# A new order of all steps for the attention and feed-forward kernel, with new places, new engines and 46 instead of 44 warm-up products

## The chip, the core and the metric

The kernel runs on one core of a Trainium2 chip. The metric is the device time of one execution in microseconds (us). Inputs and outputs are float32 and lie in HBM. The engines are TensorE (PE in the profile; its weight loads are PEld), VectorE (DVE), ScalarE (ACT), GpSimd (POOL) and SyncE (SP), whose queue issues all transfers here.

## The reference

Eight batches of eight heads have 512 tokens and 32 states each, of 64 numbers. Tokens read from states and states from tokens, each by a softmax. The 544 rows per batch (512 token reads, 32 state reads), with the heads side by side, go through a feed-forward layer of 512 to 1024 to 512 with a softmax gate and a normalisation.

```python
def _attn_ref(x, state):                     # x (8,8,512,64), state (8,8,32,64)
    scores = scale * np.matmul(x, state.transpose(0, 1, 3, 2))
    ...                                      # softmax over the states
    xread = np.matmul(a, state)
    scores2 = scale * np.matmul(state, x.transpose(0, 1, 3, 2))
    ...                                      # softmax over the tokens
    sread = np.matmul(a2, x)
    return np.concatenate([xread, sread], axis=2)

def _moe_ref(x, w_in, w_out, g_ln):          # x (4352 rows, 512)
    h = x @ w_in
    sm = softmax(h)
    solu = h * sm
    ln = (solu - mu) / np.sqrt(var + 1e-06) * g_ln
    return (ln @ w_out).astype(np.float32)
```

The rows are 8 x 544 = 4352. The weights arrive as 64-bit floats.

## The kernel before

**Tiles.** The rows are cut into 34 tiles of 128: tile t below 32 is a quarter of the tokens of batch b = t // 4, and tiles 32 and 33 are the state reads of all batches. The matrix product of the token read with the states and that with `w_in` are joined: the states are first multiplied with `w_in`, and the token tiles then need one product with the result.

**Steps.** The work is written as named steps, each a generator that issues one instruction, or a few, at each turn:

- `l` loads a piece of a weight matrix, 512 KB; pieces 0 to 7 are `w_in` (piece 2c + n is quarter c, half n), 8 to 15 are `w_out`. `cl` (ACT) and `c` (three turns: DVE, DVE, then DVE or POOL) turn a piece into 32-bit floats. `wi` and `wo` split the weights into a high and a low part.
- `Ls` loads the states of four batches, `LT` and `Ln` load the tokens of a batch in two layouts.
- `V` b n multiplies the states of batch b with half n of `w_in` (`all_heads`, L191). It has two product turns, j = 0 and j = 1 (four heads and two quarters of `w_in` each), and two evictions. One product takes 64 rows and 32 columns of TensorE's array; the four of a turn use opposite corners, and those of j = 1 use the places that j = 0 leaves (`at = (q ^ j) * NS`).
- `S` b makes the scores of batch b by the same helper, j = 0 and j = 1 in one turn. `E` and `A` (`Ah` for batch 0, in two parts) are the two softmaxes; `R` is the read of the tokens, with two product turns, a scaling on DVE (`sr`, L423) that also frees the bank of the products, and a transposing product (L430).
- `Y`, `Z` and `P` keep a state product in DRAM, load it again and split it.
- `H` t makes the hidden row (L471): for tiles 0 to 3 in plain fp32 products, for the others in three products of split parts. `C` t is the softmax gate and the statistics; `D` t transposes it through DRAM (`ut`, `back`); `T` t splits it in four copies, `uh` and `ul` for each half; `O` t is the product with `w_out` (L539), the eviction with the scale (L546 on ACT, L548 on DVE) and the store. Tile 33 goes in two halves of 256 columns.
- `K` multiplies an identity with itself (L563). It computes nothing that is used and keeps TensorE at work while it would wait.

**What sets the order.** The string `ORDER` lists the steps turn by turn (`K*2` is two turns), and `issue` takes them one after the other. Each engine, and SP's queue of transfers, executes its own instructions in that order, so that an instruction that waits holds back all that is behind it on its engine. `OPT` says with one letter per step which engine does it (a ACT, d DVE, p POOL). `PLACES` gives each tile its buffer: `k4` are 45 buffers of 4 KB per partition that everything of that size shares, `t` four and `h` twice two banks of PSUM. A tile that takes a used buffer waits until the last reader of the one before is done.

In the old order TensorE's list begins with 15 warm-up products, then the first turn of `V30`, and ends the part with batch 0 (tiles 0 to 3) with the last step of `R0`; after that come the `H` of batch 1.

Of the kernel before, what the change touches and what calls it, by code (L numbers as in the profile page):

```python
# [28 lines left out]
OPT = dict(ph=2, k4=45, direct=[0, 1], hn=[0], vh=[0, 1], ah=[0], add='dddddpppppppdpdp', whi='aaaa', wlo='pdpp',
           ev='aaaaaaaaaaaaadaaaaaaaaaaaaaaaaaa', swh='aaaaaaaadaaaaaaa', swl='ppppdppdppdppdpd', sub='dppdddpd',  # L30
           subh='ppdddpdddpdddpdd', mulh='dpdddpdddpdddpdd', mul='ppddddpp', ath='aaaaadad', alo='dpdpdppp',
           up='aaaaaaaaadadadaaadadaaddadddaddada',
           uh='aaaadadaaaaaaaaaaaaaddaadaadaaaadaaaaadadaadaaaadadadddaaaddddaadaaa',
           ul='ddddppppdpppppdppppppdppdppdppppppdppdddpppppdppdpppddppdpdppddpdddd',
           oe='aaadaaaadaaaadaaaaaaaddddaaaaaaaaa', hs='aaaaaaaa', jit=[])
# [7 lines left out]
Ah01*2 V11 Ln00 E1*2 A1*3 P10 c9 H1*2 Ah01*2 E1 P11 Lg A1 Lg*2 V41*4 H0*2 C1*2 E1 Ah01 V51 Y71 Ah01 cl11 A1 K c11 E1
E0 C1*2 Lg Ah01 K C0 P11 E1 A1 K E1 C0 A1*2 Y41 Ln11 V51*2 H3 V51 H3 C0 D1 wo6 K Y31 cl15 LT20 C0*2 C3*2 P10 V61*2 A1
V61 A1 c11 A1 R0 c8 R0 D1 R0 l13 C0 H2 K H2 E1 K*2 V61 c15 E1 C3*3 D1 D0*2 C2 D3 K C2 S2 Ln10 wo0 wo1 R0*2 H4 C2 T1 E2
A2 E2 wo2 wo1 H4*4 E1 H4 wo3 wo0 E2 H5*2 wo3 D0 H5*2 wo2 H5*2 O1*3 R1*2 O1 T1 O1 D3 O1 T1 wo4 c13*2 C2 R0 cl13 D2 T0
Y40 O0 T0*2 wo4 O0*4 c13 wo5*2 O0 wo6 Y20 wo7*2 O0 T0 T1 E2 R1 D3 T3 A2*2 C2 C1 E2 D2 LT30 LT31 O1*3 O0*6 T3*2 O1*3 C1
O1 C4 T3 C4 O3*2 D2 O3 C3 A2 O1 O3 Y60 O3*2 C5 O3*2 C4 E2 C5*2 C4*2 C5 O3*2 D4 T2*3 O3*3 S3 Y21 T2 O0 D4 LT41 A2 E3
D5*2 E3 C4 E3*2 R1 H7*3 A2*2 H6*2 C2 D4 H6*4 C6*2 O2*2 Z21 O2*2 A2 H7 D5 A3 O2*8 H7 T4 O4*2 Y70 O4 Z20 T4*2 H7 T4 R1
O4 O3 O4 A3 Ln21 C6 O4*2 P21*2 O4*4 Ln20 O4 T5*3 A2 O2 A2 O5*3 E2*3 A2 O5*3 P20 LT40 C5 P20 C6 D6*2 C7 O4 A3 C7*2 H9*2  # L50
C5 H9*4 O5*2 C9 E3*2 O4 R1 E2 C7 D7 D6 Z30 Z31 D7 LT51 T5 O5*2 C9 O5*2 C9*2 D9*2 H8*2 O5 H8*4 S4 C8 C6*2 D7 O2 R2 Y51
R2 H10*3 R2 T6*4 Y50 O5 O6 P30*2 O6 E4 C8 H10 C8 E4 C8 A4 D9 E4*2 E3 Ln40 E4 O6*4 A3 D8*2 H10 Ln30 Z40 T7*2 H11*3 T7
O6*3 C7*2 H11*2 O6*2 P31 A3 E3*2 O6 T7 O6 H10 A3*2 O6 P31 O7*5 D8 E4 O7*3 C10 T9*3 C9*2 C10 T9 R2 C8 O7*2 A4 A3*2 H11
A3*2 A4 E4 R2 C8 O7*3 O9 LT50 R2 C10*2 T8 O9*2 C11*2 A4*2 O9*2 E3 D10 Z41 O9*7 Ln31 H13*3 O9 D10 C11*2 D11*2 T8*2 O7
T8 O9 H13*3 C13 C11*2 A4*2 D10 C13 Y61 C13 O8*8 C13 D13 C13 T10*2 H12*2 D11 Z51 T11 S5 T11 P51 T11 R3*2 A5*2 O8*4 R3
H15 H12*2 T10*2 Ln41 H15*3 O8*2 H12 E5*2 D13 H12 H15 C12*2 E5 O10*2 H15 P40 O10*2 E4 C10 O10*2 C12 C10 O10 P40 O10
O11*3 O10 A4 O10 O11 C12 E5*2 O10*3 D12 C12 H14*3 LT60 R3 A4 H14*3 T11 LT61 A4 D13 T13 E4 Ln61 C15 T13*3 A4 C12 O11*2
O10 D12 O11*4 C15 O11 Z50 O13*2 C15 P41 C15 Z61 C15 O11 A5 O13 D15 R3*2 O13*6 E5 P41 O11 C14 D12 E4 C14 E5*2 C14*2
Ln51 C13 T12 O13*4 H16 T12 P50 D14 T12 H16*5 S6 C16 R4 C16 P50 R4*2 O12*3 O11 D15 D14 D15 T15 D14 O12*5 C16 LT70 A5
T12 C16 O12*2 D16*2 H17 E5 A5*2 H17 O12 H17 O12 H18 H17*2 T15 E6 T15*2 C15 T14 E6 H17 O12 H18 A5 T14 E6*3 H18*2 O14*2  # L60
Z71 O14 T14 C17 D16 O14 O13 O15*2 O12 A6 O15*2 A6*2 H18 O14 P51 Ln50 H18 wi2 E5 C14 C17 O15 C17*2 D17 C17 O14*2 Z60
O15*2 O14*3 T14 O14*2 C16 C14 O14 H19*5 O15*3 A5 O15 A5 C16 T16*4 LT71 A5 C18 E6*2 C18*3 O15 H19 A5 C18 O15 E6 D18 R4
R5*2 R4 R5 O16*3 D17*2 O16*3 C19 O16*6 A6 H21*2 wi1 wi2 R4 H21 D18 C19*2 C17 H21 C19 H21 D19 O14 T17 P61 T17*2 S7 P61
E7 R5*3 D18 H21 O16 T18 H20 P60 H20 T18 O17*2 A6 O17*3 A7 C21*2 C19 D19 O17 Ln70 O17*3 P71 A6*2 E6 C21 A7 C21 D21 D19
T19 O15 E7*3 H20*2 O18 D21 O18*2 O17 T17 O17*2 T18 T19 T18 T19 O18*2 C18 P60 C21 O17*2 C21 H20*2 T19 O18 C20 H22 A7
C20 E7*2 C20*2 A6*2 E6 D21 H22*5 O19*2 T21*2 O18*5 C20 C19 O19*3 Z70 H23 O18 H23 O19 D20 O19 O18 D20 T21 O19*2 O18
A7*2 C22 T21 C22*3 A6 D20 T20 O21 O19*3 O21 D22 H23 D22*2 T20*3 O19 H23*3 O21*3 C23*2 O21*3 O16 P70 Ln60 A7 O21 O20
O21*2 C23 Ln71 wi0 O21 H24 O20 E7*3 O20*3 H24 A6 O20 H24*2 C20 C23 H24 C22 H25 D23*2 T22*2 A7 H24 O21*2 H25*2 E7 O20*3
D23 H25 O20*2 P71 O20 H25*2 T22 C24*3 O20 O22*3 T22 C24 D24 O20 D24 O22*5 C25 O22*2 D24 P70 C24 O22 R7 C25 R7 R6*2
R7*2 C22 O19 C25*2 D25 A7 H27*5 T23 A7 O22*2 H27 O23*4 T23 O23 H26 R6 H26*5 T23 O23*2 O22 T24 A7 O24 T24 O24 O23*3 T23  # L70
O23*2 C23*2 O24*2 A7 T24 O24 C27*4 D27 D25 O24 D25 H28*3 O24*2 T24 O24*2 D27*2 O23*2 R7 C26 T25 C26 H28 C26*3 D26 C24
D26 O24*2 H28*2 T27 T25*2 O24*2 R6 H31*4 D26 O25*2 H31*2 O27*4 O25 C25*2 R6*2 T27*3 wi0 C28*4 R7 D28 O25 T26 O27*7 C27
# [9 lines left out]
PLACES = dict(
    k4='0123456789ABCDEFGHIJKLMNOPQRSTUVWXYZabcdefghi0248AIBLNOPTQScZabh6RKeg8VH7UZITiBGhNEFSb8UeAKZTY47iGUa'
       'fCMBEdPQAYI47FKi0GDfBCUaPgMLIQ7AVcJSKEdeLGHODfQiJgMCFdVYBEPefLXKSWcA4IaiQJGEDOfKCF7U0LVIcAOECWFHQDKP'
       '0LG27UVY4JeIdcPAMg0QSaXiG7YECdPfD4eg2UQBHScC7Yf2XaiO4XadeQFBLKi0VDcUAIH42GYQFK3XadgMUiDcLOAHKa2dgCGL'
       'cQPdMHiE7eBWLQKOaCgUSBcLd2PgUQS37OAJiaKF2DEMY4GIWgPBUJQ3F2LdDa1AO5Eg4iYKUMcJPLHCS7XDQa359I',
    sm='0123102310231023103210321032130213',
    o='0110110101010101011100010101101101',
    t='01231231231312312312312313123112301313021313021231023110212031312303120230123013203201230123',
    h='01100101010110101010101010101010101010')  # L90
# [554 lines left out]
```

## Time and profile before

| | |
|---|---|
| median of 3 runs | 356.75 us (356.3 to 358.56) |
| the profiled execution | 357.5 us |
| its span on the core | 355.5 us |
| TensorE products busy | 346.2 us (97%) |
| VectorE busy | 280.8 us (79%) |
| ScalarE busy | 217.2 us (61%) |
| GpSimd busy | 176.9 us (50%) |
| moved by DMA | 92.16 MB, mean 259 GB/s |

The profile is of one execution. Times in it are counted from the start of the span; the span ends with the last instruction of the program, and 2.0 us of the execution's 357.5 lie outside it. Rows of the timeline give start, duration, engine, line, operation, output and inputs, shapes and how many were merged; in brackets stands how long the engine had been idle and what ended that. Rows of products overlap each other, since the ends of products are modelled: from the start of one row to the start of the next is what a reader should count. An fp32 product is recorded two or more times.

### The profile page before, as it was taken

The page shows a single profiled execution, that of the slowest core. Times are in us where ns is not written, and L with a number is a line of the kernel's source. Part 1 is how long each engine was busy: PE and PEld are TensorE (multiplying, and loading weights), DVE is VectorE, ACT ScalarE, POOL GpSimd, SP SyncE. Part 2 cuts the span into 40 slices and gives each one's busy share as a digit, 9 for nine tenths or more (in the row PEclk, how much of TensorE's full clock was granted, in tenths as well). Part 3 has the DMA queues.
Part 4 walks back from the last instruction along what each step waited for, and adds up shares of the span by engine and source line. Part 5 has one row for each costly group of instructions (what it writes and reads, how often), then busy time and mean ns, then how long its engine had stood idle before and what let it go on. Part 6 is the DMA issues. An engine that isn't in the chain of part 4 may idle for free.

```text
span 355.5 us, 6260 instructions
## 1 busy us (share of the span) xinstructions
PE 346.2 (97%) x2304; PEld 262.0 (74%) x2304; DVE 280.8 (79%) x398; ACT 217.2 (61%) x353; POOL 176.9 (50%) x237
## 2 busy tenths in 40 slices
...
GB/s 249 414 407 347 277 201 301 346 310 306 351 285 333 363 361 324 328 283 375 348 209 280 326 192 271 205 241 165 321 224 148 207 148 89 161 165 178 117 149 60
DMA packets 47086, 92.16 MB, mean 259 GB/s; under 512 B 4176, under 2 KB 25936, under 8 KB 47056
## 3 DMA queue, kind: packets, MB, share of 16 engines
...
## 4 chain that ended last, share of the span: by engine, by line
PE 56%; DMA 6%; DVE 5%; ACT 1%; issue 0%; ACTq 0%; SPq 0%; DVEq 0%
PE o L539 37%; PE h L471 16%; DMA ut<-ub 3%; DMA back<-ut 3%; PE srps L419 1%; DVE sm L478 1%; DVE ub L508 1%; DVE u L484 1%; DVE m L380 1%; PE sps L191 1%; DVE a L375 1%; PE srT L430 1%; DVE aT L395 0%; DVE z L387 0%; DVE swl L147 0%
## 5 line engine op out<-in xcount | busy, mean ns | idle before, releaser
L147 POOL TENSOR_TENSOR ul<-back,uh 128x512 fp32r<-128x512 f32 x43 | 57.6, 1345 | 60.7 <-ACT uh L142 32.5
L539 PE MATMUL o<-wohi,uh 128*128 128x512 f32 (+1 forms) x280 | 74.2, 385 | 1.3 <-DVE sr L423 1.3
L539 PE MATMUL o<-wolo,uh 128*128 128x512 f32 (+1 forms) x280 | 74.8, 384 | 0.0
L539 PE MATMUL o<-wohi,ul 128*128 128x512 f32 (+1 forms) x280 | 74.8, 383 | 0.0
L481 ACT ACTIVATE e<-h,sm 128x1024 f32<-128x1024 f32 x34 | 37.9, 1114 | 40.0 <-DVE sm L478 39.8
L539 PEld LDWEIGHTS o<-wohi,uh 128*128 128x128 f32 x280 | 51.5, 188 | 12.2 <-DVE sr L423 1.7
L539 PEld LDWEIGHTS o<-wohi,ul 128*128 128x128 f32 x280 | 51.8, 188 | 10.4
L539 PEld LDWEIGHTS o<-wolo,uh 128*128 128x128 f32 x280 | 51.5, 188 | 10.4
L484 DVE SCALAR_TENSOR_TENSOR u<-h,e 128x1024 f32<-128x1024 f32 x34 | 41.2, 1212 | 17.2 <-ACT e L481 16.6
L508 DVE STREAM_TRANSPOSE ub<-u 128x1024 f32<-128x1024 f32 x34 | 42.2, 1242 | 7.3 <-ACT u L489 6.5
L478 DVE TENSOR_REDUCE sm<-h 128x1 f32<-128x1024 f32 x34 | 40.9, 1204 | 8.0 <-ACT osb L546 4.7
L142 ACT ACTIVATE uh<-back 128x512 fp32r<-128x512 f32 x48 | 28.9, 623 | 23.7 <-DMA back<-ut 23.5
L496 ACT ACTIVATE e<-u 128x1024 f32<-128x1024 f32 x34 | 35.8, 1053 | 9.5 <-DVE u L491 9.1
L546 ACT ACTIVATE osb<-o,sm 128x512 f32<-128x512 f32 (+1 forms) x28 | 18.6, 665 | 28.7 <-PE o L539 17.6
L471 PE MATMUL h<-swh,ath 128*128 128x512 f32 x112 | 35.1, 396 | 0.0
L471 PE MATMUL h<-swh,atl 128*128 128x512 f32 x112 | 34.7, 391 | 0.0
L471 PE MATMUL h<-swl,ath 128*128 128x512 f32 x112 | 34.6, 390 | 0.0
L489 ACT ACTIVATE u<-u,sm 128x1024 f32<-128x1024 f32 x21 | 24.1, 1148 | 12.8 <-DVE u L484 12.8
L241 POOL TENSOR_TENSOR wf<-wf,r 128x512 uint32<-128x512 uint32 x9 | 11.9, 1323 | 33.2 <-DVE wf L238 11.6
L500 POOL TENSOR_TENSOR sm<-sm 128x1 f32<-128x1 f32 x34 | 9.4, 277 | 35.4 <-ACT e L496 33.5
L147 DVE TENSOR_TENSOR ul<-back,uh 128x512 fp32r<-128x512 f32 x25 | 19.1, 780 | 7.1 <-ACT uh L142 6.8
L471 PEld LDWEIGHTS h<-swl,ath 128*128 128x128 f32 x112 | 21.0, 188 | 4.5
...
## 6 DMA issues: line engine op xcount, KB each, us to landing
ut<-ub SPq DMA_DIRECT2D x34, 512.0 KB, 3.1
back<-ut SPq DMA_DIRECT2D x34, 512.0 KB, 4.5
...
xT<-xT_dram SPq DMA_DIRECT2D x16, 512.0 KB, 6.8
xn<-xn_dram SPq DMA_DIRECT2D x16, 512.0 KB, 7.0
kept<-vt SPq DMA_DIRECT2D x12, 512.0 KB, 5.9
swf<-kept SPq DMA_DIRECT2D x12, 512.0 KB, 7.0
raw<-w_in_dram SPq DMA_DIRECT2D x8, 512.0 KB, 8.8
```

The costliest lines, as they stand in the source:

```text
L142: nc.scalar.activation(out, src, AF.Copy)
L147: engine(k).tensor_tensor(out=out, in0=a, in1=hi.bitcast(F32), op=ALU.subtract)
L241: engine(of("add", n)).tensor_tensor(out=w, in0=w, in1=rounding[n], op=ALU.add)
L471: nc.tensor.matmul(ph[t][:, cols], left[l][:, p, tok], weights[:, cols], start=(p, l, r) == (0, 0, 0), stop=(p, l, r) == (parts - 1, *kind ...
L478: nc.vector.tensor_reduce(nm, ph[t], AX.X, ALU.max, negate=True)
L481: nc.scalar.activation(e, ph[t], AF.Exp, bias=nm, accum_out=z)
L484: nc.vector.scalar_tensor_tensor(out=u, in0=ph[t], scalar=1.0, in1=e, op0=ALU.mult, op1=ALU.mult, accum_out=su)
L489: nc.scalar.activation(u, u, AF.Identity, bias=su, scale=-float(DF))
L496: nc.scalar.activation(e, u, AF.Square, scale=float(DF) ** -0.5, accum_out=ss)
L508: nc.vector.transpose(ub, us[t][0])
L539: nc.tensor.matmul(po, ut[t][l][:, f, :], w[NP + f // 2][:, f % 2, cols], start=(hf, l, w is wohi, q) == (0, 0, True, 0), stop=(hf, l, q) ...
L546: nc.scalar.activation(o[:, cols], po, AF.Copy, scale=us[t][1])
```

## The change

Every step stays what it is, and no operation is added or taken away except two turns of `K`. The whole of `ORDER`, most of `PLACES` and many letters of `OPT` are new. The strings are long; their beginnings and the end of `ORDER` show it, and below them is told what differs in words.

```diff
-OPT = dict(ph=2, k4=45, direct=[0, 1], hn=[0], vh=[0, 1], ah=[0], add='dddddpppppppdpdp', whi='aaaa', wlo='pdpp',
-           ev='aaaaaaaaaaaaadaaaaaaaaaaaaaaaaaa', swh='aaaaaaaadaaaaaaa', swl='ppppdppdppdppdpd', sub='dppdddpd',
-           subh='ppdddpdddpdddpdd', mulh='dpdddpdddpdddpdd', mul='ppddddpp', ath='aaaaadad', alo='dpdpdppp',
+OPT = dict(ph=2, k4=45, direct=[0, 1], hn=[0], vh=[0, 1], ah=[0], add='dddddpddppdppppp', whi='adaa', wlo='ppdp',
+           ev='adaaaaaaadaaaaaaaaaaaaaaaaaaaaaa', swh='aaaaaaaaaaadaaaa', swl='pppppdpppppdpdpd', sub='dppppppd',
+           subh='dpdddpdddpdddpdd', mulh='ppdddpdddpdddpdd', mul='pppppppd', ath='aaaddaad', alo='dppdpppd',
...
 ORDER = """
-l0 c0*2 K l4 c4*2 K*2 l2 K*4 cl0 c0 K*2 cl4 K*3 c2 K*3 Ls0 c2 cl2 c2 V30 K*2 c4 l6 c6 cl6 l12 c6*2 V30*2 l1 cl12 V20
-c1 K V30 V00 V20*2 V10 Ls2 K l3 V70*2 K cl1 V20 l7 cl3 c12*3 c3*2 c7 cl7 c1 c3 V70*2 c7 V10*2 V00*2 LT00 V10 LT01 c7
-V00 S0 K*2 c1 E0 l5 K*2 cl5 l8 E0 l9 Ah00 E0*2 c5 l15 Ah01 V50*3 c8 c5 c9 l14 E0*2 K*3 l10 V50 c5 K cl8 V71*2 LT10 K
+l2 cl2 c2*3 l0 cl0 l6 K c0 K*9 c0*2 K l4 cl6 K*3 c6*3 K Ls0 V30 K*3 l12 cl4 V00 l7 K c4*3 V30*2 cl12 K c12*3 c7*2 cl7
+c7 V30 V20*2 V10 V20*2 Ls2 l1 K c1*2 l3 c3 cl1 V00 V10 K V70 V00*2 K c1 LT01 c3 cl3 V10 c3 V70*3 LT00 S0 Ah00 E0*2 K*3
+l5 c5 Ah01 c5 cl5 c5 V10 Ah00 l15 E0 K*2 E0*2 Ah00 V50*2 K*2 V50*2 V11 Ah01 Ah00 l8 c8 cl8 l14 E0 Ah00 K*2 V71*4 V01*3
...
-C33*2 D33 T30 T31 T30*2 O31*2 D33 H32*2 T29 H32 T30 O31*4 H32*2 T29 H32*2 T29*2 C33*2 O28 O30*3 C32*5 D32 O30*2 O29
-O30*3 D33 T33*4 O30*4 O29*7 O33*6 C30*2 O30 D32*2 C32 O33*6 O30 O33*7 O31 O33 T32 O33*3 T32*3 O33*3 O32 O33 O32*6 O33
-O32*5 O29*3 O32*2 O29*3
+O33*2 T33*2 D32 O33 T30 C29*2 D32 O29*2 O30 O31 O33*2 O30*3 O33*2 D32 O33*2 T32*3 C33 O29 T32 O33*9 C32 O33*2 O32 O30
+O32*11 O33*7 C32 O32*2 O33
```

TensorE's own list up to the `H` of batch 1, with the turns of `V` and `S` by j:

```
before: K*15 V30.0 K*2 V30.1 V20.0 K V00.0 V20.1 V10.0 K V70.0 V70.1 K V10.1 V00.1 S0.0 S0.1 K*4 V50.0 V50.1 K*4
        V71.0 V71.1 K V11.0 V40.0 V40.1 V01.0 V01.1 V11.1 V21.0 V21.1 V31.0 K*5 V31.1 V60.0 K*2 V60.1 S1.0 S1.1
        H1 H1 V41.0 V41.1 H0 H0 V51.0 K*3 V51.1 H3 H3 K V61.0 V61.1 R0 R0 H2 K H2 K*3 S2.0 S2.1 R0 | H4
after:  K*15 V30.0 K*3 V00.0 K V30.1 K V20.0 V20.1 V10.0 K V00.1 V10.1 K V70.0 K V70.1 S0.0 S0.1 K*5 V50.0 V50.1 K*2
        V11.0 K*2 V71.0 V71.1 V01.0 V01.1 V40.0 V40.1 K V31.0 V31.1 K V11.1 K*2 V21.0 V21.1 V60.0 H1 V60.1 S1.0 S1.1
        H1 K H0 K H0 V41.0 K*4 V41.1 K*4 H3 H3 V51.0 R0 R0 V51.1 V61.0 H2 H2 V61.1 S2.0 S2.1 R0 | H5
```

The first transfers in SP's queue were pieces 0, 4, 2, the states, 6, 12, 1, the other states; they are now pieces 2, 0, 6, 4, the states, 12, 7, the other states. Between R3 and O10 DVE's list held `T10`, two turns of `A5`, the `sr` of R3; it now holds the `sr` of R3 ahead of `T11` and `T10`, and the first copy of `T10` is on ACT. TensorE's list ended with O33, then O32 and the last four turns of O29; it now ends with O32 and, behind it, the last six turns of the second half of O33. By engine and net, DVE gives up three `sub` and three `mul` of whole blocks to POOL and five `up` to ACT, and takes five `ul` from POOL; some ten single steps of other kinds change their engine too.

More of the change, by code (lines that the diff above doesn't have):

```diff
@@ L27 @@
 NTILES = B * NT + B * NS // P
-OPT = dict(ph=2, k4=45, direct=[0, 1], hn=[0], vh=[0, 1], ah=[0], add='dddddpppppppdpdp', whi='aaaa', wlo='pdpp',
-           ev='aaaaaaaaaaaaadaaaaaaaaaaaaaaaaaa', swh='aaaaaaaadaaaaaaa', swl='ppppdppdppdppdpd', sub='dppdddpd',
-           subh='ppdddpdddpdddpdd', mulh='dpdddpdddpdddpdd', mul='ppddddpp', ath='aaaaadad', alo='dpdpdppp',
[L32 to L35, printed above, removed]
@@ L37 @@
-ORDER = """
-l0 c0*2 K l4 c4*2 K*2 l2 K*4 cl0 c0 K*2 cl4 K*3 c2 K*3 Ls0 c2 cl2 c2 V30 K*2 c4 l6 c6 cl6 l12 c6*2 V30*2 l1 cl12 V20
-c1 K V30 V00 V20*2 V10 Ls2 K l3 V70*2 K cl1 V20 l7 cl3 c12*3 c3*2 c7 cl7 c1 c3 V70*2 c7 V10*2 V00*2 LT00 V10 LT01 c7
-V00 S0 K*2 c1 E0 l5 K*2 cl5 l8 E0 l9 Ah00 E0*2 c5 l15 Ah01 V50*3 c8 c5 c9 l14 E0*2 K*3 l10 V50 c5 K cl8 V71*2 LT10 K
-Ah01 Ah00*2 E0*2 c9 c14 l11 c15 Ah00 V11 V71 V40 V71 V40 Ah00*2 V40*2 V01*2 V11 LT11 cl14 V21 V11 E0 V21*3 V31 K*2
-Ln01 c15 K*3 V31*2 Y30 V60 Ah00 K*2 c10 V01*2 Ah00 c8 V31 Ah00 V60 c14 V60 S1 cl10 c10*2 V60 c14 c11 LT21 cl9 Lg
@@ L43 @@
[L43 to L72, printed above, removed]
@@ L73 @@
-O27 D28 C27 wi1 O27 H29 C31*5 O27 O25*2 T26 O26*2 D28 T26*2 H29 O25 H29*2 O25 T25 O25 H29*2 O25*2 T28 O25*2 T28*2
-D31*3 H30*2 C31 C29*4 wi3 O26*8 C26 O28 X*2 C29*2 H30*4 O26*3 D29*2 O28*2 C30*2 O28*2 T31*2 O28 H33 O28 O26 H33 C28
-H33*3 T28 H33*2 O28*4 wi3 C28 O28 H33*5 O31 C30 O28 C30 O31*3 D30 H32*2 D29 H32*2 D30*2 H32 O31*2 T31 O31 C33*2 O25
-C33*2 D33 T30 T31 T30*2 O31*2 D33 H32*2 T29 H32 T30 O31*4 H32*2 T29 H32*2 T29*2 C33*2 O28 O30*3 C32*5 D32 O30*2 O29
-O30*3 D33 T33*4 O30*4 O29*7 O33*6 C30*2 O30 D32*2 C32 O33*6 O30 O33*7 O31 O33 T32 O33*3 T32*3 O33*3 O32 O33 O32*6 O33
@@ L78 @@
-O32*5 O29*3 O32*2 O29*3
+OPT = dict(ph=2, k4=45, direct=[0, 1], hn=[0], vh=[0, 1], ah=[0], add='dddddpddppdppppp', whi='adaa', wlo='ppdp',
+           ev='adaaaaaaadaaaaaaaaaaaaaaaaaaaaaa', swh='aaaaaaaaaaadaaaa', swl='pppppdpppppdpdpd', sub='dppppppd',
+           subh='dpdddpdddpdddpdd', mulh='ppdddpdddpdddpdd', mul='pppppppd', ath='aaaddaad', alo='dppdpppd',
+           up='aaaaaaaaaaaaaaadaaaaaaadaaddaadddd',
+           uh='aaaadaaaaaaaaaaaddddaddaddaaaaaaaaaadaddadaddaadadaaaaaaaaaadddadaaa',
+           ul='dddpdddpppdppppdpppppddppppddpdddpppdddppppppdpppdddddppppdpdddpddpp',
+           oe='aaaaaaaaaaaadaaaaaaaaadaddddaaaada', hs='aaaaaaaa', jit=[])
@@ new lines @@
+ORDER = """
+l2 cl2 c2*3 l0 cl0 l6 K c0 K*9 c0*2 K l4 cl6 K*3 c6*3 K Ls0 V30 K*3 l12 cl4 V00 l7 K c4*3 V30*2 cl12 K c12*3 c7*2 cl7
+c7 V30 V20*2 V10 V20*2 Ls2 l1 K c1*2 l3 c3 cl1 V00 V10 K V70 V00*2 K c1 LT01 c3 cl3 V10 c3 V70*3 LT00 S0 Ah00 E0*2 K*3
+l5 c5 Ah01 c5 cl5 c5 V10 Ah00 l15 E0 K*2 E0*2 Ah00 V50*2 K*2 V50*2 V11 Ah01 Ah00 l8 c8 cl8 l14 E0 Ah00 K*2 V71*4 V01*3
+V40*2 c14 l9 c15 V40 Ah00 c8 Ah00*2 E0 V40 Ah01*2 E0 l10 K LT11 Lg*2 V31*2 K V11 Ah00 c10 l11 K*2 V31*2 Lg V01 cl10
+V21*3 V60 c9 H1 V21 V60*2 LT10 S1 V11*2 c10 c15 c11 Ah01 c14 Ln00 c10 H1 cl11 E0 K Lg c9 c11*2 P11 Ah01 Y31 A1 P10 E1
@@ new lines @@
+l13 E1 Ah01 Y71 H0 A1 V60 c8 Ah01 E1 K H0 cl9 V41 C1*2 K*2 A1 Lg Ln01 A1 cl15 Ah01 K cl14 LT21 K wo0 V41 E0 V41 P11
+C1*2 K*2 LT20 E1*2 C0 D1 A1*3 Y40 K*2 c14 Y21 V41 E1 D1 E1 H3 C0 C1 C0 H3 Y20 Y41 C3 V51 C0 A1*2 R0 c9 R0*2 V51*2 D0
+V61 C3*2 D0 D1 E1*2 P10 D0 H2*2 V61 C2 V51 V61 wo0 S2 A1 R0*2 H5*2 cl13 A1 H5 wo1 R0 H5*2 Ln10 H5 wo2 wo3 C2*2 wo1 E1
+Ln11 T1 O1*2 V61 C3 H4*2 c15 H4*2 wo2 H4 wo6 T1 O1 c13 wo3 c13 T0*2 H4 O0*3 D3 T1 D3 E2 Y51 c13 wo7 C2 D2*2 T1 D3 wo4
+wo5 wo4 O1*2 T0 O0*3 C3 C0 O1*3 O0 LT31 O0 wo5 O1 O0 E2 wo7 E2 wo6 O1 E2 T0 E2 O1*2 C2 O0*3 E2 A2*3 R1*2 T3 O3 LT30 C1
@@ new lines @@
+O1 O3 D2 T3*2 LT41 Z20 C0 O0*2 C5 T3 O3 C4 C5 O3*3 C5 C4 R1 LT40 Z21 C4 O3*4 T2 A2*2 T2 S3 T2*2 E3 C3 O3 H6 E3 C4 D4
+C4*2 H6*3 E2 H7 C5 D4 A2 O3 C5 O2*3 A2 Y60 O2 H6 Ln20 H6 D4 O2*8 C2 O3*2 E3*2 P20 D5*2 A2 A3 E3 H7 A3 E2 E3 C6 P21*2
+H7*4 Ln21 S4 A2 T4 O2 P20 R1 E2 C7 Z40 T4*3 C6*2 D5 O2 O1 A2 O4*2 Y61 O4*3 C7 O4*3 C6*2 O4*2 A3 H9 O4 C7*2 D6 D7 D6 H9
+C7 R1 A2 H9 Z31 T5 C5 R1 A3 D7 O4*2 H9*3 D6 H10*4 A4 O5*2 H10*2 O5 E2 O5 D7 Y30 Ln31 T5*2 C7 C9*2 A4 C9 A3*2 C9 D9
+O5*2 T5 C6 O5*2 P31 A3 O5 A3 D9 O4 A4 O5*3 E3 T6 H8 Z30 H8 O5 T6*3 A4 H8*2 C9 H8*2 E3 R2 E3 C8*2 R2*2 T7 E4 O6*8 C8
```

40 lines of the change are left out of this document (32 added, 8 removed).

## The prediction

> **What bounds the kernel now.** I read the totals first, then whom TensorE waited for, then its timeline from the start to the point where it no longer waits, and last the stretches before and after that point.
>
> ```profile
> PE 346.2 (97%) x2304; PEld 262.0 (74%) x2304; DVE 280.8 (79%) x398; ACT 217.2 (61%) x353; POOL 176.9 (50%) x237
> ```
>
> Waits of TensorE (us in total, times, longest; the one for the states stands in brackets further down), and the busy time of the engines in two stretches and the rate of the DMA in a third (us, busy and instructions by engine, clock, DMA share, GB/s):
>
> ```profile
> PE o L539 <- DVE sr L423: 1.3, 1, 1.3
> PE swps L191 <- POOL wf L241: 0.5, 1, 0.5
> PE swps L191 <- DVE a L375: 0.5, 1, 0.5
> ```
>
> ```profile
> 9.67:59.92 50.25, 49.28 (x467) 20.61 (x467) 45.15 (x78) 40.81 (x72) 23.79 (x19) 1.00 0.89 322
> 59.92:351.68 291.76, 290.50 (x1812) 235.06 (x1808) 231.57 (x314) 172.41 (x277) 152.36 (x212) 1.00 0.72 250
> ...
> 10.00:30.00 20.00, 19.03 (x201) 1.00 1.03 410
> ```
>
> TensorE sets the time. From 59.92 to 351.68 it does 290.5 us of work in 291.8, and one wait, 1.3 us, is all that a new order can take out. So what matters is when that stretch begins, whether it stays closed, and the few us after it. The stretch before it, from the first state product at 9.67, has to be taken apart (start, us, what; an instruction in fp32 counts twice or more):
>
> ```profile
> 1.35 6.46 PE L563 MATMUL warm<-ident 128*128 128x128 f32 x30 [1.35 <-POOL ident masks.py:199]
> 9.67 1.66 PE L191 MATMUL swps<-wf,st 64*32 64x512 f32 x8 [1.86 <-DMA st<-stB_dram]
> 11.26 0.71 PE L563 MATMUL warm<-ident 128*128 128x128 f32 x4
> 11.90 1.05 PE L191 MATMUL swps<-wf,st 64*32 64x512 f32 x4
> ...
> 14.47 0.49 PE L563 MATMUL warm<-ident 128*128 128x128 f32 x2
> 14.89 0.63 PE L191 MATMUL swph<-wf,st 64*32 64x512 f32 x4
> ...
> 16.74 0.49 PE L563 MATMUL warm<-ident 128*128 128x128 f32 x2
> 17.16 1.09 PE L191 MATMUL swps<-wf,st 64*32 64x512 f32 x16
> 18.18 0.49 PE L563 MATMUL warm<-ident 128*128 128x128 f32 x2
> 18.60 0.63 PE L191 MATMUL swph<-wf,st 64*32 64x512 f32 x4
> 18.73 0.63 PE L191 MATMUL sps<-xT,st 64*32 64x512 f32 x4
> ...
> 19.48 1.04 PE L191 MATMUL swph<-wf,st 64*32 64x512 f32 x8
> ...
> 21.31 1.16 PE L563 MATMUL warm<-ident 128*128 128x128 f32 x8
> 22.40 1.06 PE L191 MATMUL swps<-wf,st 64*32 64x512 f32 x8
> 23.91 1.06 PE L191 MATMUL swps<-wf,st 64*32 64x512 f32 x8 [0.46 <-DVE a L375]
> 24.91 1.16 PE L563 MATMUL warm<-ident 128*128 128x128 f32 x8
> ```
>
> ```profile
> 36.96 3.70 PE L471 MATMUL h<-swf,aT 128*128 128x512 f32 x8
> 40.59 1.09 PE L191 MATMUL swps<-wf,st 64*32 64x512 f32 x16
> ...
> 45.24 1.06 PE L191 MATMUL swps<-wf,st 64*32 64x512 f32 x8
> 46.24 0.94 PE L563 MATMUL warm<-ident 128*128 128x128 f32 x6
> ...
> 52.97 1.10 PE L419 MATMUL srps<-xn,e 128*32 128x64 f32 x64
> 53.99 1.98 PE L471 MATMUL h<-swf,aT 128*128 128x512 f32 x4
> 55.82 0.38 PE L563 MATMUL warm<-ident 128*128 128x128 f32 x2
> 56.04 1.88 PE L471 MATMUL h<-swf,aT 128*128 128x512 f32 x4
> ...
> 59.54 0.45 PE L430 MATMUL srT<-ident,sr 128*64 128x64 f32 x8
> 59.92 0.73 PE L471 MATMUL h<-swh,ath 128*128 128x512 f32 x2
> ```
>
> **Prices in this stretch.** One `V` or `S` step issues products of 64 rows by 32 columns that fill half of the array: those of j = 0 and of j = 1 lie in opposite places. V70 with both (16 records) ran from 17.16 to 18.18, 1.02; V51 with j = 0 alone (8 records) took from 45.24 to 46.24, as long. So I count rounds: in a run with nothing else between, the larger of the number of j = 0 and of j = 1. One round is 1.02; V00 j0, V20 j1, V10 j0 are two rounds and go from 14.89 to 16.74, 1.85; V10 j1, V00 j1, S0 j0, S0 j1 are three, 18.60 to 21.31, 2.71. That is 0.14 per run and 0.86 per round. A group of n warm-up products between such runs takes 0.42 for one (18.18 to 18.60) and 1.09 for four (21.31 to 22.40): 0.20 per group and 0.22 each. Beside `H` work one takes 0.22 (55.82 to 56.04). A whole `H` of tiles 0 to 3 takes 3.63 (36.96 to 40.59), half of one 1.83 (53.99 to 55.82); R0 1.02 (52.97 to 53.99) and its last step 0.38 (59.54 to 59.92).
>
> **Before, summed.** From 9.67 to 59.92 the old order has 15 runs with 23 rounds: 15 x 0.14 + 23 x 0.86 = 21.9. Ten groups of warm-up with 24 products between them: 2.0 + 5.3 = 7.3; five products in three places beside `H` work: 1.3. The four `H`, 3.6 each: 14.4. R0 and its last step: 1.4. Together 46.3; it took 50.25, so 4.0 us are waits: 0.6 in the first run (9.67 to 11.26, one round), 1.6 in the second (11.90 to 14.47, one round), 1.5 at V50 (22.40 to 24.91, one round whose halves came apart), the rest elsewhere. The waits row names only the part in which nothing at all ran.
>
> **After, summed.** *Warm-up and broken pairs.* Both orders put 15 warm-up products ahead of V30. From V30 to the end of the last step of R0 the new one has the same `V`, `S`, `H` and `R` steps, but in 19 runs with 27 rounds: V70, V11 and V41 are now split with each j by itself, V00 j0 and V30 j1 stand alone, and V00 j1 stands beside another j = 1. That is 19 x 0.14 + 27 x 0.86 = 25.9. Warm-up: 14 groups with 29 products, 2.8 + 6.4 = 9.2, and two beside `H`, 0.47. `H` 14.4, R0 1.4. Sum 51.4. So with no wait left, the stretch is 1.1 longer than the old one with its waits.
>
> *Its start.* The new order loads raw2, raw0, raw6, raw4 and then the state; the old one has the state fourth.
>
> ```profile
> 0.72 1.33 SPq L212 DMA_DIRECT2D raw<-w_in_dram  x3
> 2.09 0.53 SPq L176 DMA_DIRECT2D st<-stB_dram  x1
> ...
> st<-stB_dram SPq DMA_DIRECT2D x2, 512.0 KB, 8.8
> ```
>
> Three loads and then the state leave SP, and V30 starts as it lands. The queue moves 410 GB/s here, so one more load of 512 KB ahead is 524288 B / 410 GB/s = 1.3 us, and V30 starts near 10.95. No reason allows a gain: both need st0. The raw loads of V30's other half are then in, which is how the first two waits (2.2 us) go.
>
> *Waits that it has.* Two places look close when the lists of ACT and DVE are read beside TensorE's. V50 j1 takes the bank of S0 j0, which two DVE transposes and an ACT exponential must read first. V31 j1 takes the bank of V40 j0, whose copy on ACT stands behind those of V71 and V01. All that is queued behind both on TensorE moves with them. The bounds are 0 and the 4.0 of the old order. I take 0.8, two waits a little under the 0.5 of the two short ones in the list, and so near the lower end, because the warm-up gives the other engines 1.9 us more (9.2 for 7.3). DVE, 45.15 of the old 50.25 us busy, has nearly the same work before the end of this stretch, so it is not later than TensorE is.
>
> *The long stretch.* The work is the same, with one more change between kinds of product (0.1 to 0.3, taken as 0.2). The wait of 1.3 had this cause:
>
> ```profile
> 151.56 0.43 DVE L144 CAST uh<-back 128x512 fp32r<-128x512 f32 x1 [2.47 <-DMA back<-ut]
> ...
> 153.14 0.25 DVE L423 TENSOR_TENSOR sr<-srps,sc 128x128 f32<-128x128 f32 x1
> ```
>
> O10 takes the bank of srps3, and `sr3`, which frees it, stood on DVE behind a copy of T10 that waited for its landing. In the new list `sr3` comes ahead of T10 and T11, and T10's first copy is on ACT: -1.4 with the switch. Of the moved engines, `sub` and `mul` go from DVE to POOL in three more blocks each, five `ul` come back, and five `up` go from DVE to ACT. With DVE at 281, ACT at 217 and POOL at 177 us beside TensorE's 346, a few us either way make none of them the bound: 0.
>
> *The end.* The last product is now the second half of O33, with half the columns, and its eviction and store are short:
>
> ```profile
> 351.76 0.69 ACT osb L546
> ```
>
> ```profile
> 344.44 0.48 ACT L546 ACTIVATE osb<-o,sm 128x256 f32<-128x256 f32 x1 [0.53 <-PE o L539]
> ```
>
> 0.69 - 0.48 is a gain of 0.2, but the store of O32 is issued just ahead of it on SP: between -0.2 and +0.3, taken as -0.1.
>
> Sum: +1.3 + 1.1 + 0.8 + 0.2 - 1.4 - 0.1 = +1.9. The profiled execution took 357.5 with a span of 355.5; it would become 359.4. It lies 0.75 over the median of 356.75, so the median becomes **358.6** (with the terms' own bounds, above all 0 and 4.0 for the waits, 357.6 to 361.9).
>
> **Rivals.** *The pairs are not broken (16%).* If TensorE draws a free half round past the products between, the four extra rounds vanish: 4 x 0.86 = 3.4 less, 355.2. It decides where a lone V and its other half are parted by one warm-up product (V00, V30, V70). For it: the four sps records at 18.73 began ahead of the swph records at 19.48, although V00 j1 stands before S0 j0 in the order. Against it: a warm-up product fills the whole array, and no record here passes one. The Trainium skill ("TensorE: Matmul & The Clock Gate", Part 3, "What overlaps and what doesn't") has matmuls start and end strictly in program order; by that this rival has no chance, but the rows at 18.73 and 19.48 disagree with the page.
>
> *New waits in the long stretch (18%).* DVE is busy 231.6 of 291.8 us there. If the six `sub` and `mul` steps that went to POOL make one block's `H` late, or another copy blocks DVE's queue as T10 did, one or two waits of 1.4 follow: 360.0 or 361.4. It decides from two such waits on, which take the time past 360.3. For it: the old order had one such wait. Against it: the head comes 2 to 3 us later, and every lead grows by that.
>
> *The array goes cold (8%).* The first 15 products took 6.46 us, 0.43 each against 0.22 later: half pace. The last ends at 7.8, and V30 now waits until 10.95: a gap of 3.1 instead of 1.86. If it lets the pace fall for another 6 us, 3 us are lost: 361.6. The Trainium skill (same page, "Why this matters for your kernels") warns of idle gaps over about 3 us, after which the array runs at half rate; no gap in this trace is that long.
>
> **Numbers.** My case has 58%. Within 1% of 356.75 (353.2 to 360.3; about what can be told from no change) lie 55 of these, three quarters of the first rival (12), a third of the second (6) and a fifth of the third (2): 0.75. Faster by over 1%: a quarter of the first, where other waits go too, 0.04. Slower: 3, 12 and 6, 0.21. The range, 356.2 to 361.9, leaves out most of the first rival and a tail above.
>
> **What would show it.** V30 starts near 10.95; the first h from swh near 63 instead of 59.92; 27 rounds, with lone V steps at about 1.0; no wait of o for sr; the long stretch 290 to 291 us; after the last product 3.7. I am wrong if that stretch begins before 61, if V steps run past warm-up products, if the first V steps run at half pace, or if a wait of over 1.5 us stands in the long stretch.

## The result and the profile after

The new order is slower: 361.72 us at the median of 4 executions (361.0 to 362.98) against 357.53 for the kernel before on the same chip (4 executions, 356.3 to 358.56). The ratio is 1.0114, with a 95% interval of 1.0065 to 1.0163. The forecast of 358.6 was 3.1 too low; the range held the time. The change between the medians is +4.2 us, where +1.9 was forecast. The profiled execution took 361.0 us with a span of 359.2, 3.7 more than before. One execution of e1_filled (581.0 us) and the profiled one of e8_all_three (582.0) ran at a mean clock of 0.57 and 0.56, so the comparisons leave them out, and e8 has no usable times by stage.

The totals and the chain of the kernel after, and the granted clock over the 40 slices of its span:

```profile
PE 350.9 (98%) x2308; PEld 262.7 (73%) x2308; DVE 277.9 (77%) x396; ACT 220.3 (61%) x354; POOL 179.8 (50%) x238
...
PEclk9899999999999999999999999999999999999999
...
PE 96%; DVE 2%; DMA 1%; issue 0%; ACT 0%; DVEq 0%
```

TensorE is busy 4.7 us more (346.2 before) on two more products. Its waits, in us in total, times and longest:

```profile
PE swps L191 <- DVE wf L235: 3.0, 1, 3.0
PE warm L563 <- POOL ident masks.py:199: 1.3, 1, 1.3
```

The wait of O10 for `sr` and the two of 0.5 are gone; only the wait ahead of V30 is left, and it has grown from 1.9 to 3.0. So the listed waits are about 1 us shorter in all, and the time lost isn't in them. Busy time (instructions) of PE, PEld, DVE, ACT and POOL in the two stretches of the prediction, followed by the clock, the DMA share and GB/s:

```profile
10.86:64.64 53.78, 53.78 (x470) 21.11 (x470) 45.25 (x77) 40.12 (x70) 23.80 (x19) 0.97 0.84 312
64.64:355.28 290.64, 290.64 (x1812) 235.31 (x1808) 227.01 (x310) 175.72 (x279) 155.23 (x212) 1.00 0.70 247
```

| | before | after | change | forecast |
|---|---|---|---|---|
| V30 starts | 9.67 | 10.86 | +1.19 | +1.3 |
| V30 to the first `h` of batch 1 | 50.25 | 53.78 | +3.53 | +1.9 (1.1 + 0.8) |
| that `h` to the last product | 291.76 | 290.64 | -1.12 | -1.2 (0.2 - 1.4) |
| last product to the end of the span | 3.84 | 3.94 | +0.10 | -0.1 |
| sum | 355.5 | 359.2 | +3.7 | +1.9 |

Three lines came out within 0.2. The first stretch is 1.6 too long, and its mean clock is 0.97 where the old one had 1.00. The timeline of TensorE in it (start, us, what, how many records, and in brackets the idle time ahead):

```profile
1.35 6.46 PE L563 MATMUL warm<-ident 128*128 128x128 f32 x30 [1.35 <-POOL ident masks.py:199]
10.86 1.93 PE L191 MATMUL swps<-wf,st 64*32 64x512 f32 x8 [3.05 <-DVE wf L235]
12.71 1.62 PE L563 MATMUL warm<-ident 128*128 128x128 f32 x6
14.27 1.06 PE L191 MATMUL swph<-wf,st 64*32 64x512 f32 x8
15.26 0.49 PE L563 MATMUL warm<-ident 128*128 128x128 f32 x2
...
26.20 1.78 PE L191 MATMUL swps<-wf,st 64*32 64x512 f32 x16
27.91 0.71 PE L563 MATMUL warm<-ident 128*128 128x128 f32 x4
28.55 1.06 PE L191 MATMUL swph<-wf,st 64*32 64x512 f32 x8
29.55 0.71 PE L563 MATMUL warm<-ident 128*128 128x128 f32 x4
...
33.38 1.37 PE L191 MATMUL swps<-wf,st 64*32 64x512 f32 x16
34.68 0.49 PE L563 MATMUL warm<-ident 128*128 128x128 f32 x2
```

V30's first round takes 1.85 (10.86 to 12.71), but V00's, the same work, 0.99 (14.27 to 15.26). The three warm-up products between them take 1.56 (12.71 to 14.27); at 0.20 + 3 x 0.22 they should take 0.86. Together that is 1.56 us too much. The windows of the kernel after around it show why:

```profile
7.35:10.76 3.41, 0.46 (x4) 0.27 (x3) 3.10 (x6) 1.34 (x2) 0.00 (x0) 1.00 1.02 418
10.76:14.17 3.41, 3.31 (x14) 1.58 (x14) 3.17 (x7) 1.33 (x3) 0.09 (x1) 0.50 1.03 418
14.17:20.00 5.83, 5.83 (x55) 1.92 (x58) 3.48 (x6) 2.19 (x4) 1.42 (x1) 1.00 1.02 408
```

From 10.76 to 14.17, 3.41 us, the granted clock is 0.50, and 1.00 on both sides. In all traces here the recorded clock changes only after whole multiples of 3.41 us (3.41, 6.83 and 17.07 occur); such a stretch is called a window of the clock below. In the 3.41 us ahead TensorE was busy for 0.46. That is the rival called "the array goes cold".

### The profile page after: what moved, and what is told of

It is laid out like the page before. It is cut to its first block, busy times and chain, and to the rows that moved or that the text cites. A ratio compares the mean times of both kernels' runs of the same rounds, so it can differ in the third digit from the quotient of the medians.

```text
span 359.2 us, 6302 instructions
## 1 busy us (share of the span) xinstructions
PE 350.9 (98%) x2308; PEld 262.7 (73%) x2308; DVE 277.9 (77%) x396; ACT 220.3 (61%) x354; POOL 179.8 (50%) x238
## 4 chain that ended last, share of the span: by engine, by line
PE 96%; DVE 2%; DMA 1%; issue 0%; ACT 0%; DVEq 0%
PE o L539 52%; PE h L471 29%; PE swps L191 5%; PE warm L563 3%; PE srps L419 2%; PE sps L191 2%; PE swph L191 2%; DMA raw<-w_in_dram 1%; PE srT L430 1%; DVE wf L238 1%; DVE wf L241 1%; DVE wf L235 0%; ACT osb L546 0%; DVEq L241 0%
## 5 line engine op out<-in xcount | busy, mean ns | idle before, releaser
L147 POOL TENSOR_TENSOR ul<-back,uh 128x512 fp32r<-128x512 f32 x38 | 51.3, 1355 | 57.3 <-ACT uh L142 47.4
L489 ACT ACTIVATE u<-u,sm 128x1024 f32<-128x1024 f32 x26 | 29.9, 1148 | 14.1 <-DVE u L484 14.1
L563 PEld LDWEIGHTS warm<-ident 128*128 128x128 f32 x92 | 15.2, 242 | 14.9 <-issue 13.5
L147 POOL TENSOR_TENSOR swl<-swf,swh 128x1024 fp32r<-128x1024 f32 x10 | 24.9, 2488 | 2.2 <-ACT swh L142 2.2
L471 PEld LDWEIGHTS h<-swh,atl 128*128 128x128 f32 x112 | 21.0, 188 | 4.4
```

Of the source, the lines that this page charges most:

```text
L147: engine(k).tensor_tensor(out=out, in0=a, in1=hi.bitcast(F32), op=ALU.subtract)
L471: nc.tensor.matmul(ph[t][:, cols], left[l][:, p, tok], weights[:, cols], start=(p, l, r) == (0, 0, 0), stop=(p, l, r) == (parts - 1, *kind ...
L489: nc.scalar.activation(u, u, AF.Identity, bias=su, scale=-float(DF))
L563: nc.tensor.matmul(warm, ident, ident, start=True, stop=True)
```

## The experiments

Every kernel here computes the whole reference: `K` computes nothing that is used. Line numbers in e5, e7, e9 and e11 are one lower, those of e4 six lower, as their strings are shorter. "Head" is the stretch from V30 to the first `h` of batch 1. Intervals are of 95%.

**e1_filled: the gap ahead of V30 filled.** Of the kernel after, thirteen warm-up products more:

```diff
-cl6 K*3 c6*3 K Ls0 V30 K*3 l12
+cl6 K*3 c6*3 K Ls0 K*13 V30 K*3 l12
```

> The changed kernel with 13 more warm-up products ahead of V30, so that the gap from 7.5 to 10.86 us is filled; nothing else moves. Theory (the gap lets the array go cold): V30 still starts near 10.9, its run takes 1.0 instead of 1.85 and the three products behind it 0.86 instead of 1.56, so 1.5 us less than the changed kernel, and the granted clock is 1.00 from 10 to 15 us. Rival (the slow first steps come from data that is not there): the same run takes 1.85 again and the time does not change.

Measured: 359.5 us, from 359.4 to 359.62; 1.0066 of before (1.0043 to 1.0088). The timeline and a window (PE alone) of e1_filled:

```profile
10.93 1.06 PE L191 MATMUL swps<-wf,st 64*32 64x512 f32 x8 [1.29 <-DVE wf L235]
11.92 0.94 PE L563 MATMUL warm<-ident 128*128 128x128 f32 x6
12.78 1.06 PE L191 MATMUL swph<-wf,st 64*32 64x512 f32 x8
```

```profile
10.93:63.16 52.23, 52.23 (x470) 1.00 0.86 322
```

V30's round takes 0.99 and the three products 0.86. The head is 52.23, 1.55 less than after, and close to what the sum of the prediction gives with the waits measured (51.4 + 0.97 = 52.4). More work on TensorE made the kernel faster: the half rate is shown as the missing term. The spread of 2 us between executions of the kernel after went with it. The mean clock that is recorded for every execution fits: 0.995 for the two of the kernel after at 361.0, 0.991 and 0.990 for those at 362.98 and 362.43, and 0.997 to 1.000 in e1. By my estimate 0.0045 of 361 us is one more window at half rate (3.41 x 0.5 = 1.7 us); no profile shows where it lies.

**e2_state_fourth: the states loaded fourth, as before.**

```diff
-c0*2 K l4 cl6 K*3 c6*3 K Ls0 V30
+c0*2 K Ls0 l4 cl6 K*3 c6*3 K V30
```

> The changed kernel with the load of the states moved from fifth to fourth place, ahead of raw4. Theory: V30 starts near 9.6, 1.25 us sooner, the gap is 2.0 us long and the array stays warm (1.5 us), so 2.8 us less than the changed kernel. Rival (the head is set by DVE or by raw4, which now lands a place later): V30 j1 waits for raw4 and at most half of the 2.8 us is seen.

Measured: 361.24 us; 1.0113 (1.0075 to 1.015). V30 starts at 10.04 instead of 10.86, but the span is 359.2 as after. A wait and two windows (PE alone) of e2_state_fourth:

```profile
PE swps L191 <- DMA st<-stB_dram: 2.6, 1, 2.6
PE o L539 <- DVE uh L144: 0.5, 1, 0.5
```

```profile
6.54:9.96 3.42, 0.89 (x8) 1.00 0.91 285
9.96:13.37 3.41, 3.33 (x14) 0.50 1.02 419
```

A gap of 2.6 us also leads to one window at half rate, so my theory for this run was wrong: the head stays at 53.80. The 0.8 of the start is given back in the long stretch (291.41 for 290.64); the wait of an `o` (O32, for `uh` of T32), which the kernel after doesn't have, is 0.5 of it. The rest I can't place.

**e3_pairs: three broken pairs joined.** The warm-up products that part V00 j0 from V30 j1, the halves of V70 and those of V41 are moved to one side; none is taken away.

```diff
-l12 cl4 V00 l7 K c4*3 V30*2 cl12
+l12 cl4 V00 l7 c4*3 V30 K V30 cl12
-V00 V10 K V70 V00*2 K c1 LT01
+V00 V10 K*2 V70 V00*2 c1 LT01
-V41 C1*2 K*2 A1 Lg Ln01 A1 cl15 Ah01 K cl14 LT21 K wo0 V41 E0 V41
+V41 C1*2 A1 Lg Ln01 A1 cl15 Ah01 cl14 LT21 wo0 V41 K*4 E0 V41
```

> The changed kernel with the warm-up products between the halves of V70 and of V41, and between V00 j0 and V30 j1, moved to before or behind them; as many products as before. Theory (rounds count): three rounds of 0.86, three runs of 0.14 and three groups of 0.20 fewer, 3.6 us less if no other engine is late, and the long stretch begins near 61.0 instead of 64.6. Rival (other engines set the end of the head): the products of H3 or H5 wait instead, and less than 1 us is gained.

Measured: 358.63 us; 1.0039 (1.0012 to 1.0065); head 51.08, 2.7 less than after. The timeline of e3_pairs at S0:

```profile
20.70 1.09 PE L191 MATMUL swps<-wf,st 64*32 64x512 f32 x16
21.58 1.96 PE L191 MATMUL sps<-xT,st 64*32 64x512 f32 x16
23.47 1.38 PE L563 MATMUL warm<-ident 128*128 128x128 f32 x10
```

V70 and S0 are two rounds by themselves, but run from 20.70 to 23.47, 2.77, about three: half of S0 takes the bank of a V70 half that has just been written and must be copied out. The half rate is in this run too, from 10.84 to 14.26, so the 2.7 comes on top of what e1 gains. So joined pairs do save their rounds, and part of that becomes a wait further on.

**e4_before_t10_act: in the kernel before, one letter.** The first copy of T10 goes to ACT, so that DVE doesn't hold up `sr` of R3.

```diff
-uh='aaaadadaaaaaaaaaaaaaddaadaadaaaa...
+uh='aaaadadaaaaaaaaaaaaaadaadaadaaaa...
```

> The kernel before with one letter changed: the first copy of T10 on ACT instead of DVE. Theory (DVE's queue stood behind that copy, and with it sr3): the wait of o for sr is gone and the time is 1.3 us lower, near 0.996 of before. Rival: ACT's queue stands behind the copy instead and something else waits as long, or the next late input of O10 takes its place (its data were there 1.5 us ahead of need, so that is not expected at once): no change.

Measured: 356.65 us; 0.9991 (0.9966 to 1.0016). Waits and two windows (PE alone) of e4_before_t10_act:

```profile
PE swps L185 <- DMA st<-stB_dram: 2.3, 1, 2.3
PE h L465 <- DVE u L478: 0.9, 1, 0.9
PE sps L185 <- DMA xT<-xT_dram: 0.7, 1, 0.7
PE o L533 <- ACT uh L136: 0.4, 1, 0.4
```

```profile
6.68:10.09 3.41, 1.08 (x9) 1.00 0.95 377
10.09:13.51 3.42, 3.42 (x14) 0.50 1.02 417
```

The wait for `sr` is gone, yet the long stretch is 291.99, no shorter than 291.76: two others of 0.9 and 0.4 stand where it stood. The run is inconclusive on the whole, since its profiled execution also fell to half rate after a gap of 2.3 us, which the one of the kernel before didn't after 1.9. The profile of e6 further down says more about this wait.

**e5_filled_no_warm: only the gap filled.** As e1, and the 31 warm-up products from V30 on taken out.

```diff
-K Ls0 V30 K*3 l12 cl4 V00 l7 K c4*3 V30*2 cl12 K c12*3
+K Ls0 K*13 V30 l12 cl4 V00 l7 c4*3 V30*2 cl12 c12*3
...
```

> The kernel with the filled gap, and without the 31 warm-up products behind the first V30. Theory (TensorE itself sets the head of the new order, so that warm-up products there cost their own time): 31 x 0.22 + 14 x 0.20 = 9.6 us of TensorE time go, halves of V70 and V41 meet again (2.0 us more), and the head ends at least 4 us sooner than with the gap filled (355 us or less). Rival (the products only fill time in which DVE, ACT or transfers are late): waits appear in their place and the time stays within 1.5 us of 359.5.

Measured: 354.45 us (354.12 to 355.29); 0.9929 (0.9911 to 0.9947), 5.0 less than e1. Its longest wait, and a window (PE alone) behind it:

```profile
PE sps L190 <- DMA xT<-xT_dram: 4.1, 1, 4.1
```

```profile
21.71:28.54 6.83, 5.83 (x51) 0.50 1.04 394
```

TensorE now waits 4.1 us for the tokens of batch 0 and then runs two windows at half rate, and still the head takes 46.83 for 52.23. Without the warm-up products behind V30 the new order is faster than the kernel before. The 5.0 is not their price alone: with them gone the halves of V70 and V41 run side by side again, and the half rate at S0 is new.

**e6_before_filled and e7_before_filled_no_warm: the same two edits in the old order.** First nine products ahead of V30; then, with these, the 29 later ones taken out.

```diff
-c2 K*3 Ls0 c2 cl2 c2 V30 K*2 c4
+c2 K*3 Ls0 c2 cl2 c2 K*9 V30 K*2 c4
```

```diff
-c2 K*3 Ls0 c2 cl2 c2 V30 K*2 c4 l6 c6
+c2 K*3 Ls0 c2 cl2 c2 K*9 V30 c4 l6 c6
...
```

> The kernel before with 9 more warm-up products ahead of V30, so that its gap of 1.9 us is filled. Theory (the half-rate window falls by chance on the first V steps of some executions of the kernel before, depending on where the clock's windows lie): the lower end stays near 356.3 and the executions at 358 to 360 become rare, median 0.3 to 1 us lower. Rival (the spread has another cause): the spread stays at 356.2 to 359.

> The kernel before with the filled gap and without the 29 warm-up products behind the first V30. Theory (its head already holds 4 us of waits, DVE is 45 of 50 us busy): of the 8.6 us taken out at most 4 come back, 352.5 to 355. Rival (all of it is filler): no change from the kernel with the filled gap, near 356.4.

Measured: 357.01 (356.19 to 359.76; ratio 1.0009, 0.9984 to 1.0033) and 357.5 (356.6 to 360.01; 1.0006, 0.9979 to 1.0032). Filling the gap doesn't narrow the old kernel's spread, which so has other causes. Its executions fall to half rate too: 16 of the 24 in this comparison have a mean clock of 0.995 or less, against 0.997 to 1.000 in all of e6, so the profiled one of the kernel before, at 1.000, isn't typical in this. But the old order loses little by it, since e6 is no faster. Taking out 29 products gains nothing there. The longest waits of e7's profiled execution (359.83 us, one of its slow end):

```profile
PE swps L190 <- DVE a L374: 2.0, 1, 2.0
PE h L470 <- DVE u L483: 1.9, 2, 1.0
PE sps L190 <- DMA xT<-xT_dram: 1.9, 2, 1.4
```

These waits brought the clock down as well. Two windows (PE alone) of e7_before_filled_no_warm:

```profile
20.31:23.72 3.41, 1.09 (x16) 1.00 1.01 406
23.72:30.55 6.83, 5.34 (x48) 0.50 1.03 411
```

The head is only 1.5 shorter than that of e6 (49.06 for 50.58), and the long stretch of this execution is 4.6 longer (295.07 for 290.43). So in the old order most of what the products took came back as waits and as half rate, while in the new one the head ended 5.4 sooner. What the old order would take without them at full clock, no run shows: the clock of e7's ten executions is 0.985 to 0.990.

**e8_all_three and e10_filled_pairs: do the gains add up?** e8 is the kernel after with the states fourth, nine products ahead of V30 and the pairs joined; e10 has thirteen products and the pairs, and leaves the states fifth.

```diff
-c0*2 K l4 cl6 K*3 c6*3 K Ls0 V30 K*3 l12 cl4 V00 l7 K c4*3 V30*2 cl12
+c0*2 K Ls0 l4 cl6 K*3 c6*3 K*10 V30 K*3 l12 cl4 V00 l7 c4*3 V30 K V30 cl12
...
```

```diff
-cl6 K*3 c6*3 K Ls0 V30 K*3 l12 cl4 V00 l7 K c4*3 V30*2 cl12
+cl6 K*3 c6*3 K Ls0 K*13 V30 K*3 l12 cl4 V00 l7 c4*3 V30 K V30 cl12
...
```

> The changed kernel with three edits together: the states loaded fourth, the gap filled with 9 products, and the three pairs of halves joined. Theory: the sum of the parts, -1.5 (half rate), -1.0 (states), -2.7 (pairs) from 361.0, so 355.5 to 356.5, at or under the kernel before. Rival (behind the first V steps another engine binds once TensorE is sooner): 357.5 or more.

> The changed kernel with the gap filled and the three pairs joined, the states still fifth. Theory (the two add up): 1.5 and 2.7 us from 361.0, 356.8. Rival (what the pairs gain holds only while the first steps are slow and other engines get ahead): 358 or more, as with all three edits.

Measured: 358.32 (1.0023, 0.9998 to 1.0048) and 357.69 (357.62 to 357.94; 1.0004, 0.9983 to 1.0026). They don't add up. Of e10_filled_pairs:

```profile
PE sps L191 <- DMA xT<-xT_dram: 0.9, 1, 0.9
```

Once the head is quick enough, S0 waits for the tokens, and that is as much as e10 lacks to the 356.8 expected. e8, whose states are loaded sooner, is no faster than e10.

**e9_warm_at_S0: products only where TensorE waits.** As e5, with sixteen products ahead of S0.

```diff
-V70*3 LT00 S0 Ah00 E0*2 l5
+V70*3 LT00 K*16 S0 Ah00 E0*2 l5
```

> The kernel with the filled gap and no later warm-up, with 16 warm-up products in the one place where TensorE then waited longest: the 4.1 us ahead of S0, which needs xT0. Theory (that wait let the array go to half rate from 21.7 to 28.5 us, over V50, V11, V71, V01 and V40, which then took about twice as long): S0 still starts near 21.1, the granted clock stays 1.00, and 2 to 3 us go, 351.5 to 352.5. Rival (the V steps behind S0 wait for DVE and ACT and their pace matters little): less than 1 us, near 354.

Measured: 353.56 us (353.3 to 353.72); 0.9889 (0.9854 to 0.9925): faster than both kernels. The two stretches of e9_warm_at_S0 (columns as for the kernel after), and its timeline at S0:

```profile
10.87:56.52 45.65, 42.71 (x441) 17.10 (x441) 43.38 (x76) 38.12 (x69) 21.86 (x18) 1.00 0.93 348
56.52:347.85 291.33, 291.08 (x1812) 235.17 (x1808) 227.45 (x311) 177.21 (x280) 158.30 (x214) 1.00 0.71 250
```

```profile
16.84 3.84 PE L562 MATMUL warm<-ident 128*128 128x128 f32 x32
20.98 1.20 PE L190 MATMUL sps<-xT,st 64*32 64x512 f32 x16 [0.30 <-DMA xT<-xT_dram]
21.84 1.06 PE L190 MATMUL swps<-wf,st 64*32 64x512 f32 x8
24.77 0.63 PE L190 MATMUL swps<-wf,st 64*32 64x512 f32 x4 [1.86 <-ACT e2T L352]
```

The clock is 1.00 throughout, and the wait for the tokens shrinks from 4.1 to 0.3. The head gains 1.2, less than I expected: a wait of 1.9 for the exponential of batch 0 on ACT, 1.0 in e5, takes the rest.

**e11_states_warm_at_S0: and the states fourth.** Nine products ahead of V30, sixteen ahead of S0, no others.

```diff
-c0*2 K l4 cl6 K*3 c6*3 K Ls0 K*13 V30 l12
+c0*2 K Ls0 l4 cl6 K*3 c6*3 K*10 V30 l12
```

> As the kernel with 16 products at S0, with the states loaded fourth and 9 instead of 13 products in the first gap. S0 waits for xT0, which lands at the same time whichever of the first five loads is the states. Theory (the start of V30 is cover for that wait): no change from the kernel with 16 products at S0, within 0.5 us. Rival (the start carries through, as the prediction had it): 1 us lower.

Measured: 354.64 us (353.36 to 354.79); 0.9907 (0.9874 to 0.9941), no better than e9. Two of its five executions took 353.4, as e9 does; the profiled one is of the three at 354.6 to 354.8. V30 starts 1.0 sooner (9.86), the head takes 1.4 longer (47.09), and the long stretch has a new wait:

```profile
PE swps L190 <- ACT e2T L352: 1.9, 1, 1.9
...
PE o L538 <- ACT uh L141: 1.1, 1, 1.1
```

What V30 gains is lost at its own second half: the `wf` of raw4, which is now loaded behind the states, isn't ready, and TensorE waits 1.3 us for it (from 11.8 to 13.0). So S0, behind the same sixteen products, starts at 21.42, 0.4 later than in e9, and the wait for ACT at V50 is 1.9 as there.

## Why the prediction was right and wrong

**Wrong: that the array stays at full pace.** The rival "the array goes cold" came true, inside an otherwise right sum. I gave it 8% and priced it at another 6 us at half pace. It took one window of 3.41 us, and cost 1.55 us (the head is 52.23 in e1 for 53.78); that the first V steps run at half pace is one of the signs that the prediction named against itself. The step that failed: the sum lengthens the gap ahead of V30 to 3.1 us and has no term for what the gap does to the clock. I asked only whether it passes 3 us. In the records, what goes with the drop is how little ran in one window (0.46, 0.89 and 1.08 us of 3.4 were followed by half rate). The sentence "no gap in this trace is that long" kept me from seeing that the old gap of 1.86 was close as well. The window of the kernel before around it (PE alone; the clock's record begins at 7.33 in this trace and at 7.35 in that of the kernel after):

```profile
7.33:10.74 3.41, 1.55 (x11) 1.00 1.02 417
```

There 1.55 of 3.41 us were busy and the clock stayed. The rule of the Trainium skill ("TensorE: Matmul & The Clock Gate", "Why this matters for your kernels") spoke against the change and was right in kind; the gap of 3.05 agrees with its 3 us, but those of 2.6 (e2) and 2.3 (e4) don't.

**Luck: that the range held.** Its upper end of 361.9 was there for waits of up to 4.0 us, and these came out at 0.97; the terms' own bounds, added up, even give 362.3. What took the time to 361.72 was the half rate, which had no term, and a median of the kernel before that was 0.8 higher in this comparison (357.53 for 356.75), neither of which the range was made for.

**Right: the start.** +1.19 for +1.3. What I didn't see is that it's worth little by itself: e2 and e11 load the states fourth again and are no faster.

**Right: broken pairs and warm-up.** Lone `V` rounds took 0.99 to 1.00 (14.27 to 15.26, 21.62 to 22.62, 28.55 to 29.55), so the rival in which they slip past warm-up products fell. With the half rate gone (e1) the head is 52.23, and the forecast's 51.4 + 0.8 is 52.2.

**Right: the two bank waits.** V50's run took 1.71 (26.20 to 27.91) and V31's 1.30 (33.38 to 34.68), where a run of one round takes 1.02: 0.69 + 0.28 = 0.97, at the places named, for 0.8.

**Right in size, not shown in cause: the long stretch.** -1.12 for -1.2, and no wait for `sr`. But e6 has no wait there either, though its order behind V30 is the old one and `sr` of R3 still stands behind the copy of T10. A window and a row of e6_before_filled:

```profile
60.35:350.78 290.43, 290.40 (x1812) 1.00 0.71 251
150.11 0.43 DVE L144 CAST uh<-back 128x512 fp32r<-128x512 f32 x1 [1.00 <-DMA back<-ut]
```

There the data of T10 let the copy start at 150.11, in the profile before at 151.56. So the wait comes and goes between executions of one order. The stretch took 290.6 in four profiles of the new order (after, e1, e3, e10) and 291.3 to 292.0 in four others (e2, e5, e9, e11), so a difference of 1.1 between two profiles can't be put down to the order; e4 shows besides that to remove that wait alone isn't enough. The rival of new waits there fell: the list of the kernel after has none.

**The end.** +0.10 for -0.1. The eviction is shorter as forecast, 0.47 for 0.69, in the chain of the kernel after:

```profile
355.32 0.47 ACT osb L546
```

From its end to the end of the span it takes 3.4 us (359.2 - 355.79), before 3.05 (355.5 - 352.45). The two last stores stand close together on SP, which is likely the cause; no run tried it.

**Left out: what the warm-up products cost.** I priced both orders with them and never asked for the price of the new order without. e1 against e5 puts it at 5.0 us, the pairs that they part included; that is more than the whole change of 4.2.
